# Second layer in Strassen form for all groups, banks seeded by copies, and a searched order of instructions, in an attention and gated two-layer kernel

## The chip, the cores and the metric

One core of a Trainium2 chip runs the whole program. The metric is the device time of one execution in microseconds (us), lower is better. TensorE does the matmuls, VectorE and ScalarE the element-wise work, GpSimd some conversions and the issue of stores, SyncE the issue of most loads. In profile lines they are PE (and PEld for its weight loads), DVE, ACT, POOL and SP; a q behind a name (SPq) is that engine's sequencer, which issues transfers. Most executions of a kernel agree within some tenths of a per cent; single ones are slower, and a run over 1.5% above the fastest of its kernel counts as slow.

## The reference

```python
# q, k, v: (8 batches, 8 heads, 576 positions, 64), float32
def phi(x, c, s):                        # c, s: cosine and sine of the position
    r = np.maximum(x, 0.0)
    return np.concatenate([r * c, r * s], axis=-1)
kv  = einsum('bhsf,bhsd->bhfd', k_p, v)           # k_p = phi(k), q_p = phi(q)
z   = sum(k_p, axis=2)
num = einsum('bhsf,bhfd->bhsd', q_p, kv)
den = einsum('bhsf,bhf->bhs', q_p, z) + 1e-6
x   = (num / den), heads merged                   # (4608, 512)
h   = x @ w_in                                    # 512 -> 2048
out = (h * cos(h)) @ w_out                        # 2048 -> 512
```

The 4608 rows are taken in nine groups of 512: the first 512 positions of each of the eight batches, and one group "r" gathered from what is left over of all batches. Attention of a batch makes the x of its group. Layer 1 is x @ w_in with the gate, layer 2 is the product with w_out.

## The kernel before

Every piece of work is an operation with the engines that may do it, an estimated time for each, a priority, dependences, and slots of buffer rings that it takes or gives back. A list scheduler, run while the program is built, picks the next operation and fixes both its engine and its place. On the chip each engine then does its own line strictly in that order.

```python
t0, e0 = min((c[0], c[1]) for c in cand)           # earliest start over all candidates
t, _, us, o, _ = min((c for c in cand if c[1] == e0 and c[0] <= t0 + self.EPS),
    key=lambda c: (c[4] if e0 == "DMA" else 0.0, c[3].prio, c[0]))
```

A batch begins with its features, phi of k and q. They read buffers of which there is one per tensor (k, q, v), so the next batch's loads start when the last feature has read its buffer. For the first batches VectorE or ScalarE does a k feature:

```python
kf[(t, g)] = op({"A": 0.68, "V": 0.46} if cut or not g else {"A": 0.68},   # cut: batches 0, 1
    (2, b, 1), lambda e, t=t, g=g: feat(e, b, "k", t, g),
    deps=[ka, land[(b, "k", 0)]], rel=[sl["raw_k"]])
```

Layer 2 of group 0 is plain, 64 matmuls of 512 columns:

```python
def layer2_plain(base):
    for t in T:                                     # four tiles of 128 rows
        h1 = op({"PE": 1.73}, base(t, 0), lambda t=t: plain2(t, range(NJT // 2)),
                deps=d + w_land[NG:NG + NG // 2], acq=[s], rel=[g_slot[0]])
        h2 = op({"PE": 1.73}, base(t, 1), ..., deps=[h1] + w_land, rel=[g_slot[0]])
        c = op({"A": 0.6, "V": 0.69}, ..., ev, deps=[h2] + ...)     # copy to the output tile
```

The other eight groups use a Strassen form (Winograd's): seven products of half size in place of eight, in three PSUM banks X, Y and Z, with sums of gates (s) and of weights (WT) made by VectorE. The first product (X) is needed in three results, so it is saved, and added to the others from there:

```python
p1 = product(0, [], gates, [sX])
e1 = op({"A": 0.6}, EV, lambda e: cp(e, part(g, "s1"), ps[(g, "X")]), deps=[p1], acq=[s1])
p6 = product(1, wsum, S_(1), [sY])
e6 = op({"V": 0.69}, EV, lambda e: add(part(g, "u2"), g, "Y", "s1"), deps=[p6, e1], ...)
# ... p2, p7, p5, p4, p3, with three more additions of this kind on VectorE
```

Of the kernel before, what the change touches and what calls it, by code (L numbers as in the profile page):

```python
# [14 lines left out]

class Slot:


    def __init__(self, ring, n=1):
        self.ring, self.left, self.end = ring, n, 0.0  # L20


def flat(x):
    return tuple(z for y in x for z in flat(y)) if isinstance(x, tuple) else (x,)


class Op:
    def __init__(self, alts, prio, fn, deps, lat, acq, rel, at):
        self.alts, self.prio, self.fn, self.deps, self.lat = alts, flat(prio), fn, deps, lat
        self.acq, self.rel, self.at, self.end = acq, rel, at, None  # L30


class Plan:


    SEM, EPS = 0.08, 0.1

    def __init__(self, rings):
        self.ops, self.free = [], {r: [0.0] * n for r, n in rings.items()}
# [6 lines left out]
    def run(self, cold=0.0):  # L46
        users, wait = {}, {}
        for o in self.ops:
            wait[o] = len(o.deps)
            for d in o.deps:  # L50
                users.setdefault(d, []).append(o)
        ready = [o for o in self.ops if not wait[o]]
        clock, order = {}, []
        while ready:
            cand = []
            for o in ready:
                t = max([o.at] + [d.end + d.lat for d in o.deps])
                if any(not self.free[s.ring] for s in o.acq):
                    continue
                for s in o.acq:  # L60
                    t = max(t, min(self.free[s.ring]))
                for e, us in o.alts.items():
                    cand.append((max(t, clock.get(e, 0.0)), e, us, o, t))
            if not cand:
                left = [(o.prio, o.alts, [s.ring for s in o.acq if not self.free[s.ring]],
                         [(d.prio, d.alts) for d in o.deps if d.end is None][:3])
                        for o in self.ops if o.end is None]
                raise RuntimeError("no operation can start: " + repr(left[:12]))
            t0, e0 = min((c[0], c[1]) for c in cand)
            t, _, us, o, _ = min(  # L70
                (c for c in cand if c[1] == e0 and c[0] <= t0 + self.EPS),
                key=lambda c: (c[4] if e0 == "DMA" else 0.0, c[3].prio, c[0]))
            if e0 == "PE" and t < cold:
                us *= 1.7
            for s in o.acq:
                self.free[s.ring].remove(min(self.free[s.ring]))
            o.end = t + us + (self.SEM if us else 0.0)
            clock[e0] = t + us
            for s in o.rel:
                s.left, s.end = s.left - 1, max(s.end, o.end)  # L80
                if not s.left:
                    self.free[s.ring].append(s.end)
            order.append((t, len(order), o, e0))
            ready.remove(o)
            for u in users.get(o, ()):
                wait[u] -= 1
                if not wait[u]:
                    ready.append(u)
        assert len(order) == len(self.ops)
        order.sort(key=lambda x: x[:2])  # L90
        return [(o, e) for _, _, o, e in order]
# [3 lines left out]
def kernel(  # L95
# [50 lines left out]
    WT = cpool.tile([P, 4, HJ, HM], F16, name="WT")  # L146
# [4 lines left out]
    kvzs, kps, qps, qTs, qTr, x16s, xts, gts, sms, osts, ps = ({} for _ in range(11))  # L151
    T, T1 = range(NT), range(NT + 1)
    HS = [slice(0, HB), slice(HB, H)]
    RING = {"m1": 4, "l2": 2, "at": 1}
# [20 lines left out]
    def feat(eng, b, name, t, g, hs=ALLH):  # L175
        dst = (kps if name == "k" else qps)[b][:, t, hs, g, :]
        src, sc = raw[name][:, hs, t, :], CS[:, b % 2, g, t:t + 1]
        if eng == "A":
            nc.scalar.activation(out=dst, in_=src, func=AF.Relu, scale=sc)  # L179
        else:  # L180
            (nc.vector if eng == "V" else nc.gpsimd).tensor_scalar(  # L181
                out=dst, in0=src, scalar1=0.0, scalar2=sc, op0=ALU.max, op1=ALU.mult)
# [10 lines left out]
    def q_tiles(b):  # L193
        qps[b] = apool.tile([P, NT + 1, H, 2, D], F16, name=f"qp{b}", tag="qp", bufs=1)

    def qT_tiles(b):
        qTs[b] = apool.tile([P, NT, H, P], F16, name=f"qT{b}", tag="qT", bufs=1)

    def qR_tiles(b):
        qTr[b] = apool.tile([P, H, P], F16, name=f"qR{b}", tag="qR", bufs=2)  # L200

    def qT(b, t):
        return qTs[b][:, t] if t < NT else qTr[b]
# [27 lines left out]

    def ratio(b, t, tile_, hbs):
        nb, h0 = len(hbs), hbs[0] * HB
        den = apool.tile([P, nb, HB], F32, name=f"den{b}_{t}", tag="den")
        nc.vector.tensor_scalar_add(out=den, in0=tile_[:, :, :, D], scalar1=1e-6)
        rec = apool.tile([P, nb, HB], F32, name=f"rec{b}_{t}", tag="rec")
        nc.vector.reciprocal(out=rec, in_=den)  # L237
        if hbs[0] == 0:
            x16s[(b, t)] = apool.tile([P, H, D], F16, name=f"x16{b}_{t}", tag="x16", bufs=4)
# [19 lines left out]

    def transposes(key, tag, srcs_, **kw):  # L260
# [4 lines left out]
    def q_src(b, t, h):  # L265
        return qps[b][:, t, h].rearrange("p g d -> p (g d)")

    def q_trans_dma(b, t):
        nc.sync.dma_start_transpose(  # L269
            out=qT(b, t), in_=qps[b][:, t].rearrange("p h g d -> p (h g d)"))  # L270
# [12 lines left out]

    def sin(key):
        ps[("ch", key)] = apool.tile([P, SM], F32, name="ch", tag="ch", bufs=4)
# [4 lines left out]
    def gate(key, dst):  # L290
        m = ps[key]
        nc.vector.tensor_tensor(  # L292
            out=dst, in0=m, in1=ps[("ch", key)].rearrange("p (j s) -> p j s", s=m.shape[2]),
            op=ALU.mult)
# [4 lines left out]
    def s_tiles(g):  # L299
        sms[g] = gpool.tile([P, 2, HJ, HT], F16, name=f"s{g}", tag="s")  # L300

    def sums(g, c, n):
# [3 lines left out]
        a12, s1, s2 = gv[:, 1, js, 0:HT], sms[g][:, 0, js], sms[g][:, 1, js]  # L306
        out, in0, in1, op = ((s1, a21, a22, ALU.add), (s2, s1, a11, ALU.subtract),
                             (a21, a11, a21, ALU.subtract), (a12, a12, s2, ALU.subtract))[n]
        nc.vector.tensor_tensor(out=out, in0=in0, in1=in1, op=op)  # L309

    def weight_sum(n):
        wv = w_out_sb.rearrange("p (j e) m -> p e j m", e=2)
        b11, b12 = wv[:, 0, :, 0:HM], wv[:, 0, :, HM:Dm]
        b21, b22 = wv[:, 1, :, 0:HM], wv[:, 1, :, HM:Dm]
        x, y = ((b12, b11), (b22, WT[:, 0]), (b22, b12), (b21, WT[:, 1]))[n]
        nc.vector.tensor_tensor(out=WT[:, n], in0=x, in1=y, op=ALU.subtract)

    def prod(g, n, c):
        gv = gts[g].rearrange("p (j e) s -> p e j s", e=2)
        sv, wv = sms[g], w_out_sb.rearrange("p (j e) m -> p e j m", e=2)  # L320
        lo, hi, ml, mh = slice(0, HT), slice(HT, SM), slice(0, HM), slice(HM, Dm)
        bank, first, lhs, rhs = (
            ("X", True, gv[:, 0, :, lo], wv[:, 0, :, ml]),
            ("Y", True, sv[:, 1], WT[:, 1]),
            ("X", False, gv[:, 1, :, lo], wv[:, 1, :, ml]),
            ("Y", False, gv[:, 0, :, hi], WT[:, 2]),
            ("Z", True, sv[:, 0], WT[:, 0]),
# [469 lines left out]
```

## Time and profile before

| | before |
|---|---|
| the 3 runs | 301.12, 303.61 and 308.33 us (the last counts as slow) |
| span of the profiled run | 298.7 us |
| TensorE busy | 280.1 us, 94% |
| VectorE, ScalarE, GpSimd busy | 233.7, 175.6, 102.0 us |

This is the chain of waits of the kernel before from 27 to 54 us (start, length, what):

```profile
27.75 9.18 PE M L279 x84
36.93 6.91 PE M L376 x32
...
47.45 3.45 PE M L376 x16
50.90 1.21 PE KV L219 x40
52.11 0.41 PE N L228 x12
52.52 1.74 PE M L376 x8
```

Only TensorE stands in it: layer 1 of group 0 (L279), its plain layer 2 (L376), and in the middle of that, at 50.90, the kv matmuls of batch 1. The rows of batch 1's k features (name, count, shortest, median and longest ns, first and last start) show who prepared them:

```profile
L181 DVE TENSOR_SCALAR kp<-km,CS x6: 470/482/617, 45.5 to 48.3; 128x512 f16<-128x512 f32 x6
L179 ACT ACTIVATE kp<-km,CS x4: 706/706/722, 45.5 to 47.7; 128x512 f16<-128x512 f32 x4
```

Six on VectorE and four on ScalarE begin when k has landed (45.4), are done at 48.7, and TensorE never waits for them.

### The profile page before, as it was taken

The page shows a single profiled execution, that of the slowest core. Times are in us where ns is not written, and L with a number is a line of the kernel's source. Part 1 is how long each engine was busy: PE and PEld are TensorE (multiplying, and loading weights), DVE is VectorE, ACT ScalarE, POOL GpSimd, SP SyncE. Part 2 cuts the span into 40 slices and gives each one's busy share as a digit, 9 for nine tenths or more (in the row PEclk, how much of TensorE's full clock was granted, in tenths as well). Part 3 has the DMA queues.
Part 4 walks back from the last instruction along what each step waited for, and adds up shares of the span by engine and source line. Part 5 has one row for each costly group of instructions (what it writes and reads, how often), then busy time and mean ns, then how long its engine had stood idle before and what let it go on. Part 6 is the DMA issues. An engine that isn't in the chain of part 4 may idle for free.

```text
span 298.7 us, 6583 instructions
## 1 busy us (share of the span) xinstructions
PE 280.1 (94%) x2565; PEld 201.3 (67%) x2565; DVE 233.7 (78%) x450; ACT 175.6 (59%) x303; POOL 102.0 (34%) x107
## 2 busy tenths in 40 slices
PE   8879999899969987999979999999999999999993
PEld 8768856688855555566646666776666666566782
DVE  1878888899995798887869798987786786768661
ACT  2846748599379797679489497634433443443210
POOL 1370004396191686287077194011002001100500
PEclk9979999999999999999999999999999999999998
DMA  7799995897899999999999999715202100200213
GB/s 218 264 163 203 204 362 183 279 308 120 273 274 235 356 232 169 283 278 203 322 256 202 238 369 195 141 47 151 35 0 94 48 1 32 111 2 0 91 52 140
DMA packets 77086, 53.29 MB, mean 178 GB/s; under 512 B 46080, under 2 KB 74752, under 8 KB 77056
## 3 DMA queue, kind: packets, MB, share of 16 engines
q1 hardware_dynamic: 69760, 39.73, 55.2%
q0 software_dynamic: 6848, 12.59, 16.6%
q10 hardware_dynamic: 448, 0.57, 0.5%
q8 instruction: 20, 0.33, 0.5%
q14 instruction: 10, 0.08, 0.1%
HBM read 36.74 MB, written 9.44 MB: 155 GB/s over the span
## 4 chain that ended last, share of the span: by engine, by line
PE 55%; DMA 16%; DVE 10%; POOL 5%; SPq 5%; ACT 4%; issue 3%; ACTq 0%; DVEq 0%
PE M L279 26%; DMA vm<-in_v_dram 13%; PE PY L337 8%; PE PZ L337 6%; PE PX L337 5%; PE M L376 5%; POOL qp L181 4%; DMA qm<-in_q_dram 3%; PE KV L219 2%; DVE g L292 2%; SPq L171 2%; DVE x L241 2%; PE TP L263 2%; DVE s L309 2%; SPq L269 1%
## 5 line engine op out<-in xcount | busy, mean ns | idle before, releaser
L279 PE MATMUL M<-xT,w_in_sb 128*128 128x512 f16 (+1 forms) x640 | 120.2, 336 | 2.9 <-ACT xT L159 2.6
L286 ACT ACTIVATE ch<-M 128x512 f32<-128x512 f32 x144 | 84.9, 595 | 60.8 <-PE M L279 58.7
L292 DVE TENSOR_TENSOR g<-M,ch 128x512 f16<-128x512 f32 x128 | 85.8, 687 | 27.0 <-ACT ch L286 26.1
L279 PEld LDWEIGHTS <-w_in_sb 128*128 128x128 f16 x704 | 67.3, 98 | 46.6 <-issue 3.1
L181 POOL TENSOR_SCALAR qp<-qm,CS 128x512 f16<-128x512 f32 x29 | 60.0, 2074 | 31.0 <-DMA qm<-in_q_dram 27.0
L337 PEld LDWEIGHTS <-g 128*128 128x128 f16 x560 | 54.1, 98 | 11.5
L369 POOL DMA_DIRECT2D out_dram<-ost x14 | 7.8, 558 | 98.6 <-DVE ost L351 42.5
L179 ACT ACTIVATE kp<-km,CS 128x512 f16<-128x512 f32 x52 | 35.1, 715 | 0.2
L179 ACT ACTIVATE qp<-qm,CS 128x512 f16<-128x512 f32 x40 | 26.9, 713 | 11.9 <-DMA qm<-in_q_dram 11.9
L337 PE MATMUL PX<-w_out_sb,g 128*128 128x256 f16 x224 | 27.6, 273 | 0.0
L241 DVE TENSOR_TENSOR x<-N,rec 128x512 f16<-128x512 f32 (+1 forms) x44 | 26.1, 594 | 1.7 <-DVE rec L237 0.2
L337 PE MATMUL PY<-WT,g 128*128 128x256 f16 x224 | 27.2, 273 | 0.0
L337 PEld LDWEIGHTS <-s 128*128 128x128 f16 x224 | 21.4, 98 | 7.1 <-DVE s L309 2.8
L161 POOL CAST V<-vm 128x512 f16<-128x512 f32 (+1 forms) x22 | 13.9, 664 | 15.9 <-DMA vm<-in_v_dram 15.9
L228 PE MATMUL N<-kvz,qT 128*128 128x65 f16 x256 | 14.7, 196 | 2.3 <-DVE x L241 2.1
L228 PEld LDWEIGHTS <-qT 128*128 128x128 f16 x256 | 12.6, 100 | 6.1 <-issue 3.5
L337 PE MATMUL PY<-WT,s 128*128 128x256 f16 x112 | 14.1, 273 | 2.2 <-DVE s L309 2.2
L181 DVE TENSOR_SCALAR kp<-km,CS 128x512 f16<-128x512 f32 x28 | 15.5, 590 | 0.3 <-DMA km<-in_k_dram 0.2
L292 DVE TENSOR_TENSOR gr<-M,ch 128x512 f16<-128x512 f32 x16 | 10.9, 689 | 5.7 <-ACT ch L286 5.5
L219 PE MATMUL KV<-V,kp 128*128 128x65 f16 x320 | 12.9, 196 | 2.5 <-DVE kp L181 0.7
L279 PE MATMUL M<-xR,w_in_sb 128*128 128x512 f16 x64 | 15.1, 379 | 0.0
L219 PEld LDWEIGHTS <-kp 128*128 128x128 f16 x320 | 11.7, 99 | 4.7 <-issue 2.4
(70 smaller groups left out, 287.7 us busy)
## 6 DMA issues: line engine op xcount, KB each, us to landing
out_dram<-ost POOLq DMA_DIRECT2D x28, 256.0 KB, 4.1
qm<-in_q_dram SPq DMA_DIRECT2D x8, 640.0 KB, 5.3
km<-in_k_dram SPq DMA_DIRECT2D x8, 640.0 KB, 7.0
qm<-in_q_dram SPq DMA_DIRECT2D x8, 512.0 KB, 5.8
km<-in_k_dram SPq DMA_DIRECT2D x8, 512.0 KB, 8.8
vm<-in_v_dram SPq DMA_DIRECT2D x6, 640.0 KB, 8.1
vm<-in_v_dram SPq DMA_DIRECT2D x6, 512.0 KB, 8.9
w_in_sb<-in_moe_w_in_dram POOLq DMA_DIRECT2D x4, 512.0 KB, 9.0
```

The costliest lines, as they stand in the source:

```text
L161: (nc.vector if eng == "V" else nc.gpsimd).tensor_copy(out=out, in_=in_)
L179: nc.scalar.activation(out=dst, in_=src, func=AF.Relu, scale=sc)
L181: (nc.vector if eng == "V" else nc.gpsimd).tensor_scalar(out=dst, in0=src, scalar1=0.0, scalar2=sc, op0=ALU.max, op1=ALU.mult)
L219: nc.tensor.matmul(tile_[:, n, hh, :], lhsT=kps[b][:, t, h].rearrange("p g d -> p (g d)"), rhs=V1[:, t, h, :], start=(t == 0), stop=(t == NT))
L228: nc.tensor.matmul(tile_[:, n, hh, :], lhsT=qT(p, t)[:, h, :], rhs=kvzs[p][:, h, :], start=(i == 0), stop=(i == len(parts) - 1))
L241: nc.vector.tensor_tensor(out=dst, in0=tile_[:, :, :, 0:D], in1=rec.unsqueeze(3).broadcast_to((P, nb, HB, D)), op=ALU.mult)
L279: nc.tensor.matmul(ps[key][:, n, :], lhsT=w_in_sb[:, c, j * P:(j + 1) * P], rhs=x[:, c, s0:s1], start=(c == 0 and n == 0), stop=(c == NCT ...
L286: nc.scalar.activation(out=ps[("ch", key)], in_=ps[key].rearrange("p j s -> p (j s)"), func=AF.Sin, bias=math.pi / 2.0, scale=1.0)
L292: nc.vector.tensor_tensor(out=dst, in0=m, in1=ps[("ch", key)].rearrange("p (j s) -> p j s", s=m.shape[2]), op=ALU.mult)
L337: nc.tensor.matmul(ps[(g, bank)][:, i, :], lhsT=lhs[:, j, i * P:(i + 1) * P], rhs=rhs[:, j], start=(first and i == 0 and j == 0), stop=(j ...
L369: e0.dma_start(out=five[:, t0:t0 + 2, :], in_=blocks(ost, n))
L376: nc.tensor.matmul(ps[("M2", t)], lhsT=gts[0][:, j, t * P:(t + 1) * P], rhs=w_out_sb[:, j, :], start=(j == 0), stop=(j == NJT - 1))
```

## The change

The intent: fewer matmuls (group 0 in Strassen form too), less VectorE work for the evacuation of the products (a copy of X into the bank Y, onto which the next products are added), finer buffer rings for q, and an order of all operations found offline by annealing in place of the scheduler. The description of the change also says that GpSimd runs no two-input operation; that was true of the kernel before as well. Layer 1 stays plain; code for a Strassen form of it is there, unused, but three of its sums over w_in are still computed.

```diff
-    def run(self, cold=0.0):
-        ... (the list scheduler)
+    def run(self):
+        return [(self.ops[int(x.rstrip("VAG"))], x.lstrip("0123456789"))
+                for x in ORDER.split()]
+ORDER = """
+115 22 25 230 180 184 883 818 24 229 342 21 40A 41V 42A 60 43V 44A 61V 62 45A 63V 64 38A 32V 36V
+ ... (1351 tokens: operation number and engine)
 # rings
-    "qp": 1, "qT": 1, "x16": 4, "ch": 4, "s": 2
+    "qp": 4, "qT": 4, "x16": 3, "ch": 3, "s": 3          # q by single blocks, x16 one fewer
 # evacuation of X into Y
-        p1 = product(0, [], gates, [sX])
-        e1 = op({"A": 0.6}, EV, lambda e: cp(e, part(g, "s1"), ps[(g, "X")]), ...)
+        def y_seed(e):
+            if g == 0:
+                cp(e, part(g, "p1"), ps[(g, "X")])
+            else:
+                ps[(g, "Y")] = ppool.tile([P, 2, HM], F32, name="SD", tag="l2", bufs=2)
+                cp(e, ps[(g, "Y")], ps[(g, "X")])
+        y1 = op(CP, EV, y_seed, deps=[p1], acq=[sY] if g else [q1])
 # group 0
-    layer2_plain(lambda t, n: (1, 1, t, n))
+    wsum1 = []
+    for n in range(3):                                   # read by nobody: layer 1 is plain
+        wsum1.append(op(WSUM, (1.6, n), lambda e, n=n: w_in_sum(e, n), ...))
+    layer2(0, lambda i: (1, 1, i))
```

Besides, the last product of the last group is split into two halves, each with its own copy and stores, and some denominators and value conversions go to other engines.

## The prediction

> **What bounds the kernel now.** I read the busy table and the 40 slices first, then the window table, then the chain of waits, then the wait lists, then the groups by shape. The busy table:
>
> ```profile
> PE 280.1 (94%) x2565; PEld 201.3 (67%) x2565; DVE 233.7 (78%) x450; ACT 175.6 (59%) x303; POOL 102.0 (34%) x107
> ```
>
> TensorE (PE) is far ahead, but its ends are modelled, so I priced it by start-to-start times. The chain of waits of the last third gives them, since PE follows itself there without a hole:
>
> ```profile
> 46.56 0.89 PE TP L263 x16
> ...
> 117.90 1.21 PE KV L219 x40
> ...
> 209.59 1.75 PE PY L337 x16
> 211.34 1.73 PE M L279 x8
> ```
>
> So a 512-column matmul costs 1.73/8 = 0.216 us, a 256-column one 1.75/16 = 0.109, a 65-column attention matmul 1.21/40 = 0.030, a transpose 0.89/16 = 0.056. From the first KV matmul at 13.13 us (timeline) the counts are 512 of the first kind, 1152 of the second, 640 of the third and 100 of the fourth: 110.7 + 125.6 + 19.2 + 5.6 = 261.1 us of work. PE's last matmul ends at about 293.95, so 280.8 us pass: PE has 19.7 us of holes. The same subtraction by stretch puts 6.1 of them at 13 to 30, 2.4 at 50 to 60, 6.5 at 80 to 120, 2.7 at 140 to 160, 1 at 160 to 200 and none after 200. The window table shows the same places (columns: width, then busy of PE, PEld, DVE, ACT, POOL):
>
> ```profile
> 13.00:30.00 17.00, 13.92 (x163) 11.84 (x162) 13.86 (x42) 9.89 (x19) 7.28 (x12) 0.90 1.01 163
> 30.00:50.00 20.00, 20.00 (x149) 13.04 (x147) 17.81 (x30) 13.68 (x23) 3.89 (x10) 1.00 1.05 279
> 50.00:60.00 10.00, 8.68 (x136) 6.69 (x134) 7.61 (x31) 6.07 (x13) 2.79 (x3) 1.00 0.69 217
> 60.00:80.00 20.00, 20.00 (x229) 17.85 (x227) 19.30 (x36) 15.50 (x28) 12.18 (x9) 1.00 0.90 219
> 80.00:120.00 40.00, 34.39 (x348) 23.04 (x346) 33.12 (x63) 32.32 (x56) 25.92 (x17) 1.00 1.12 256
> ...
> 200.00:280.00 80.00, 80.00 (x558) 53.24 (x556) 58.91 (x93) 33.04 (x56) 7.71 (x16) 1.00 0.16 50
> ```
>
> From 200 on PE is saturated: only fewer matmuls help there. Before 200 it waits now and then for attention, and PE's wait list names single waits, not a steady one:
>
> ```profile
> PE N L228 <- DVE x L241: 2.8, 2, 2.1
> PE M L279 <- ACT xT L159: 2.6, 1, 2.6
> PE PY L337 <- DVE s L309: 2.2, 2, 1.6
> PE TP L263 <- ACT xT L159: 1.5, 4, 0.5
> ```
>
> (Total us, times, longest.) Each is a place where an engine's order was unlucky. After the last matmul come one VectorE (DVE) addition, 293.98 to 294.67, and the last stores, to 298.73.
>
> **What the Trainium skill says.** "TensorE: Matmul & The Clock Gate", section "Wait — 56ns, not 53.3ns?", gives N / 2.4 GHz + about 2.5 ns warm, which is 215.8 and 109.2 ns: the trace agrees (216 and 109). "VectorE: DVE Perf Modes", section "The perf-mode tier table", holds any tensor_tensor with a PSUM operand at one element a cycle: the additions on PSUM take 687 ns for 512 elements, and a PSUM copy 678, so turning an addition into a copy on DVE saves nothing; only moving it to ScalarE (ACT) does (595 ns). "PSUM — Partial Sum Buffer", section "The four PSUM rules", says that ACT and DVE writes do not set the has_written bits, so a seeded bank is added to only where an earlier matmul left them set. The trace before has no seeding. The change fits the rule: group 0 alone starts its Y bank with a matmul and adds the first product by an instruction, and its products leave both banks of that ring fully written. "GPSIMD Engine Reference", section "Engine selection", makes two-input work on GpSimd (POOL) about twice as slow; the trace has none there, before or after, so that phrase of the change removes nothing.
>
> **The change part by part** (counts from the built order of both kernels, durations from the rows of before).
>
> *Group 0's second layer becomes Strassen.* 64 matmuls of 512 columns (13.8 us) give way to 112 of 256 (12.2): PE 261.1 -> 259.5 us, -1.6. It brings 8 sums to DVE (about 0.70 us each, 5.6).
>
> *Evacuation by seeding.* 40 additions on PSUM (27.5 us of DVE) become 19 (13.1), and 10 copies on ACT with 2 on DVE plus 8 saved first products become 5 + 17 + 2 half + 8 on ACT and 14 on DVE (9.5 us). ACT +12 copies and two half ones, 8 us; DVE -14.4 + 9.5 - 1.4 = -6.3.
>
> *Rest of DVE.* Three sums over w_in of 128x2048 are still built, though the plain first layer never reads them: +3.7 us of dead work at 1.22 each. The weight sums are cut in halves, about +0.5. Seventeen denominators go to ACT, -2.7; six value casts leave, -2.6; five q and one k feature come, +3.1. Sum over all parts: 5.6 - 6.3 + 3.7 + 0.5 - 2.7 - 2.6 + 3.1 = +1.3, so DVE stays near 235.
>
> *ACT and POOL.* ACT: 15 k features leave (-10.7), 4 q features (+2.9), copies +8, seventeen denominators (estimate 0.2 each, +3.5), four value casts (+2): near 181. POOL: 29 features become 34 at 2.07 us, near 112. None becomes the bound by sum.
>
> *Finer rings.* The feature tile of q was one buffer of five blocks, so the next batch's features waited for all five transposes; it becomes four single-block buffers, likewise the transposed tile. The row of POOL features had 27.0 us idle behind q loads, so this slackens the loop of features, transposes and loads. Worth nothing by itself; it lets the order be better.
>
> *Searched order.* This is the main term, since it goes at the 19.7 us. Nothing in the profile gives its size; I take it by stretch. 13 to 30: 6.1 -> 5, because the first loads end this wait. 50 to 60: 2.4 -> 3.5, worse: up to the end of batch 1's ratios DVE must now do about 4 us more (group 0's sums and the dead w_in sums come before), and it had 17.81 of 20 busy at 30 to 50. 60 to 120: 6.7 -> 2.5, single waits that an order can move. 140 to 200: 3.7 -> 1. After 200: 0 -> 0.6, because the last group's seed copy and two additions sit in line between its products (0.69 each, with about one 0.87 us product to cover each). Sum 19.7 (with 0.8 of scatter) -> 12.6 to 13.4: -6.7.
>
> *The tail.* The last evacuation becomes a half copy (estimate 0.4 us, from the 387 ns of the 128x260 ACT copies) in place of 0.69, and the last store is 128 KB, whose median landing is 2.0 us against 2.4 and 3.0 for 256 KB: -1.0. Two filler matmuls at PE's end (0.43) lie beside the store.
>
> Sum: -1.6 - 6.7 - 1.0 = -9.3 us of the 298.7 us span, 289.4, a ratio of 0.969. On the median of 303.61 that is 294; the median holds one slow draw (308.33), and on the mean of the other two, 302.4, it is 293. The search could do better than my cautious split, so I say 292.
>
> **The rivals.** *The order removes nearly all holes.* For it: holes are few and single, ACT and POOL have room, and DVE's average after 200 is 59 of 80. Holes of 4 us would give 261 - 1.6 + 13.1 + 4 + 3.1, about 280 us of span, 285 measured. Against: an order searched offline rests on fixed durations, and DMA landings vary (v loads took 7 to 12 us in the chain).
>
> *DVE becomes the bound before 120.* It has 19.30 of 20 busy at 60 to 80, more work is put just before, and a fixed order makes every engine wait for a late one. The gain of the order would go into PE waits on group 0's sums and batch 1's ratios: holes stay near 19, the rest gives -2.6, some 301 measured: same.
>
> *DMA sets attention's pace.* The mean share of the queues is 1.1 of capacity at 80 to 160 and a v load of 10.5 us is in the chain. The bytes do not change, so waits on loads would stay. Against: the transfers end at about 190 while PE works on to 294, so they are ahead on average. This too would keep about 6 us of holes, some 298 measured.
>
> *A longer dependency through the seed.* The copy must end before the next product of X and before the first of Y. With first-layer matmuls between, it is hidden; if the order packed it too tightly, 9 groups of 0.5 us would add 4.5.
>
> **Range and chances.** 292, with 286 to 299 for 8 in 10: the lower end has holes of some 7 us, the upper nearly all of them kept. Faster by over 2% means under 297.5: holes must fall by about 4 us or more together with the two sure terms. I give that 0.77, within 2% 0.20, slower 0.03, the last only if the fixed order falls out of step.
>
> **What would show it.** Right: 1264 matmuls of 256 columns and 448 of 512; PE's idle time between 60 and 200 at half or less; DVE near 235, ACT near 181; the end of PE to the end of the span about 1 us shorter. Wrong: PE waiting on sums or ratios of DVE between 40 and 70 for more than 4 us; waits of PE on seeded banks in every group; waits on loads that are as long as before. If the holes stay and the time falls, or they go and it does not, my account of the bound is wrong.

## The result, and the profile after

The changed kernel took 313.53 us (median of 4, 312.30 to 313.61) against 302.4 for the kernel before (mean of its two fast runs, 301.12 and 303.61; 305.67 and 308.33 count as slow): ratio 1.036, 95% interval 1.0275 to 1.0444. It is slower. (A ratio is the mean time of one kernel's fast runs over that of the other's fast runs in the same rounds, so it is not quite the quotient of the medians.) The profiled execution: span 310.2 us, 11.5 more than before.

The busy table after:

```profile
PE 281.8 (91%) x2615; PEld 205.1 (66%) x2615; DVE 233.6 (75%) x440; ACT 180.3 (58%) x326; POOL 111.7 (36%) x114
```

The sums are those foreseen: VectorE 233.6 (235 predicted), ScalarE 180.3 (181), GpSimd 111.7 (112). The work did not grow, so the time is in holes of TensorE. I took them as in the prediction: the time between the starts of two matmuls, less the price of the first by its width; a hole is counted in the stretch in which that first matmul begins. The whole program, from its first matmul, is then 270.4 us of work and 22.4 of holes before, 269.2 and 35.6 after:

| stretch, us | holes before | predicted after | measured after |
|---|---|---|---|
| 0 to 13 | 3.1 | not given | 4.6 |
| 13 to 30 | 6.1 | 5 | 6.3 |
| 30 to 50 | 0.1 | no change | 5.4 |
| 50 to 60 | 2.4 | 3.5 | 2.8 |
| 60 to 120 | 6.7 | 2.5 | 4.5 (3.3 to 80, 1.2 after) |
| 120 to 140 | 0.0 | no change | 1.5 |
| 140 to 200 | 3.7 | 1 | 8.4 (6.2 of it after 160) |
| 200 to the end | 0.2 | 0.6 | 2.1 |

The window table of the changed kernel for the stretches that answer to those shown of before:

```profile
30.00:50.00 20.00, 16.32 (x139) 13.73 (x138) 14.79 (x25) 9.16 (x17) 1.42 (x6) 0.91 1.07 265
50.00:60.00 10.00, 8.09 (x111) 6.79 (x109) 8.83 (x17) 9.74 (x18) 2.21 (x7) 1.00 0.01 2
...
80.00:120.00 40.00, 39.43 (x417) 29.08 (x416) 35.70 (x66) 26.43 (x52) 18.71 (x16) 1.00 1.02 235
```

From 80 to 120 PE is busy 39.43 of 40 where it had 34.39: the search did fill the holes that it was made for. From 30 to 50 PE fell from 20.00 to 16.32, and so did VectorE (17.81 to 14.79) and ScalarE (13.68 to 9.16). No engine is the bound there; they wait for each other. From 50 to 60 ScalarE has 9.74 of 10, and the transfers move 2 GB/s where they moved 217: no load of batch 2 is under way. PE's list of waits names the largest:

```profile
PE N L256 <- DVE x L276: 5.7, 3, 4.7
PE PX L430 <- DMA w_out_sb<-in_moe_w_out_dram: 3.0, 1, 3.0
PE TP L303 <- ACT qp L209: 2.1, 3, 1.2
PE KV L247 <- ACT kp L209: 1.9, 4, 1.0
```

The chain of waits says how these hang together. It is the answer to the six lines of before, from 20 to 68 us:

```profile
20.63 22.09 DMA w_out_sb<-in_moe_w_out_dram
...
42.77 1.34 PE PX L430 x6
...
44.13 0.61 ACT p L189
...
50.98 1.22 ACT kp L209 x2
...
53.42 3.68 ACT kp L209 x6
...
57.15 0.66 PE KV L247 x16
...
59.96 1.23 ACT qp L209 x2
...
61.21 0.60 SPq L201
...
61.85 5.71 DMA qm<-in_q_dram
```

Where only PE stood before, there is now the last quarter of w_out, a copy of X by ScalarE, eight k features of batch 1 on ScalarE, batch 1's kv matmuls, its last q features, the issue of batch 2's q load at 61.2 (51.4 before), and that load. The rows of the features:

```profile
L209 ACT ACTIVATE kp<-km,CS x8: 711/712/714, 50.9 to 56.4; 128x512 f16<-128x512 f32 x8
L211 DVE TENSOR_SCALAR kp<-km,CS x2: 481/482/482, 54.2 to 54.6; 128x512 f16<-128x512 f32 x2
```

Two on VectorE, eight on ScalarE, the last done at 57.1 in place of 48.7. Layer 1 of group 1 began at 66.4 us, not 58.3. Most of these 8.1 us stay: layer 1 of group 2 began at 97.6 against 89.9, 7.7 later.

The 5.4 us of holes at 30 to 50 come before all this. From start to start, 3.2 of them are the wait for the last quarter of w_out, which the first product of group 0 reads, 1.0 is a wait for the copy of X, and the remaining 1.2 are matmuls that the trace shows at half the clock (0.5 from 42.9 to 46.3 us), right after the long wait.

### The profile page after: what moved, and what is told of

Its sections match the earlier page's. It is cut to its first block, busy times and chain, and to the rows that moved or that the text cites. A ratio compares the mean times of both kernels' runs of the same rounds, so it can differ in the third digit from the quotient of the medians.

```text
span 310.2 us, 6724 instructions
## 1 busy us (share of the span) xinstructions
PE 281.8 (91%) x2615; PEld 205.1 (66%) x2615; DVE 233.6 (75%) x440; ACT 180.3 (58%) x326; POOL 111.7 (36%) x114
## 4 chain that ended last, share of the span: by engine, by line
PE 60%; DMA 20%; ACT 6%; DVE 3%; issue 1%; SPq 1%; POOL 0%; ACTq 0%; DVEq 0%
PE M L319 29%; PE SD L430 11%; PE PX L430 9%; DMA xT<-x 9%; DMA w_out_sb<-in_moe_w_out_dram 7%; PE PZ L430 7%; PE KV L247 3%; ACT kp L209 3%; DMA km<-in_k_dram 2%; DMA qm<-in_q_dram 2%; PE N L256 1%; ACT qp L209 1%; DVE g L332 1%; DVE x L276 1%; ACT ch L381 1%
## 5 line engine op out<-in xcount | busy, mean ns | idle before, releaser
L430 PEld LDWEIGHTS <-g 128*128 128x128 f16 x640 | 61.9, 99 | 20.4 <-issue 7.3
L211 POOL TENSOR_SCALAR qp<-qm,CS 128x512 f16<-128x512 f32 x20 | 42.0, 2106 | 40.7 <-DMA qm<-in_q_dram 22.8
L430 PE MATMUL PX<-w_out_sb,g 128*128 128x256 f16 x256 | 34.4, 280 | 4.1 <-DMA w_out_sb<-in_moe_w_out_dram 3.0
L465 POOL DMA_DIRECT2D out_dram<-ost x14 | 7.8, 560 | 76.2 <-ACT ost L189 55.2
L209 ACT ACTIVATE qp<-qm,CS 128x512 f16<-128x512 f32 x44 | 29.9, 713 | 6.9 <-DMA qm<-in_q_dram 6.9
L211 POOL TENSOR_SCALAR kp<-km,CS 128x512 f16<-128x512 f32 x14 | 29.3, 2105 | 3.1 <-DMA km<-in_k_dram 2.7
L430 PEld LDWEIGHTS <-s 128*128 128x128 f16 x256 | 24.5, 98 | 4.7 <-issue 0.2
L209 ACT ACTIVATE kp<-km,CS 128x512 f16<-128x512 f32 x37 | 24.5, 711 | 2.5 <-DMA km<-in_k_dram 2.5
L430 PE MATMUL PZ<-w_out_sb,g 128*128 128x256 f16 x128 | 16.6, 273 | 0.0
L430 PE MATMUL PZ<-WT,s 128*128 128x256 f16 x128 | 16.3, 273 | 0.0
L430 PE MATMUL SD<-WT,g 128*128 128x256 f16 x112 | 14.5, 273 | 0.7 <-ACT ost L189 0.7
```

Of the source, the lines that this page charges most:

```text
L209: nc.scalar.activation(out=dst, in_=src, func=AF.Relu, scale=sc)
L211: (nc.vector if eng == "V" else nc.gpsimd).tensor_scalar(out=dst, in0=src, scalar1=0.0, scalar2=sc, op0=ALU.max, op1=ALU.mult)
L430: nc.tensor.matmul(ps[(g, bank)][:, i, :], lhsT=lhs[:, j, i * P:(i + 1) * P], rhs=rhs[:, c * HJ // 2 + j], start=(first and i == 0 and j = ...
L465: e0.dma_start(out=five[:, t0:t0 + 2, :], in_=blocks(ost, n))
```

## The experiments

Eighteen kernels ran. All outputs are right. I name them by their labels and give the median and the ratio to the kernel before. The runs came in several calls, in which the fast runs of the kernel before had medians of 301.8 to 304.7 us, so where two kernels of different calls are compared, the difference of the ratios (1% is 3.0 us) is the fairer one; I give it beside the medians. An interval that reaches below 1.02 leaves open whether a kernel is slower by 2%; one that stays above 1 says that it is slower. In the diffs, letters behind an operation number are engines (A ScalarE, V VectorE).

### First round: which part costs

**greedy**: the changed kernel's operations, ordered by the scheduler of before.

```diff
-class Plan: ... return tokens of ORDER
+class Plan: ... the list scheduler of the kernel before
```

> The changed kernel's operations, tiles and rings, but the order made by the scheduler of the kernel before instead of the searched list. Theory A (the searched order does not fit the chip): 293 to 302 us, PE holes after 13 us at 20 or less. Theory B (the parts themselves, Strassen in group 0, seeding, dead sums, overload DVE early): 308 or more. Theory C (the x16 ring cut from four to three buffers stalls DVE on transposes): 305 to 310, with DVE waiting on transposes for several us again.

326.5 us (three fast runs), ratio 1.083 [1.0742, 1.0923]. The profiled execution itself: 1642 us, so its trace is not used. The searched order is worth some 13 us to these operations (326.5 to 313.5; 14 by the ratios); the operations themselves are what the old scheduler cannot place.

**x16_4**: one more buffer for the normalised x, in the searched order.

```diff
-"x16": 3,
+"x16": 4,
```

> The changed kernel with the x16 ring at four buffers again, the same searched order. Theory C: the 4.7 us PE wait on a ratio at about 172 us and the 5.4 us DVE wait on a transpose go, 305 to 308 us. Theory A in its general form (any slip makes a hole somewhere): part of it comes back elsewhere, 309 to 312. Theory B: 312 to 314.

309.96 us, 1.029 [1.0212, 1.0368]: 3.6 us less by the medians, 2 by the ratios. In the changed kernel the largest single wait lies at 160 to 180 us. PE's and VectorE's lists of waits for that window:

```profile
PE N L256 <- DVE x L276: 4.7, 1, 4.7
```

```profile
DVE x L276 <- DMA xT<-x: 5.4, 1, 5.4
```

VectorE could not write x because all three buffers were held by transposing transfers, and PE waited behind it. With four buffers that wait is nearly gone, but the holes of the stretch only fell from 6.2 to about 5.2 (and those from 180 to 200 rose by 1.2), because in ScalarE's line a k feature now waits for its load with cosines behind it (lists of ScalarE and PE, same window):

```profile
ACT kp L209 <- DMA km<-in_k_dram: 4.2, 1, 4.2
```

```profile
PE M L319 <- DVE g L332: 3.0, 2, 2.4
```

So its gain need not be from this stretch at all: layer 1 of group 1 began 1.8 us earlier (64.6) in this run. The interval overlaps that of the changed kernel.

**no_dead**: the three unread sums over w_in left out.

```diff
-lambda e, n=n: w_in_sum(e, n)
+lambda e: None
```

> The changed kernel without the three sums over w_in that nobody reads, the same searched order. Theory B: 309 to 311, since DVE gets 3.7 us back where batch 1 needs it. Theories A and C: 312 to 314.

309.53 us, 1.0278 [1.0193, 1.0363]: 4.0 us less by the medians, 2.5 by the ratios. The three sums of 1.22 us stand in VectorE's line from 55 us on, between a transposed copy, sums and ratios that others wait for, so they are not beside other work. The intervals of the two kernels overlap here too. Layer 1 of group 1 begins at 63.6, 2.8 earlier, but some of that is luck: the last quarter of w_out landed at 41.1 in this run, at 42.7 in that of the changed kernel, and batch 1's features, which stand ahead of the dead sums, ended at 54.2 instead of 57.1.

**strassen0**: the kernel before, with Strassen form in group 0. The weight sums that it needs got an earlier priority (0.9 for 1.5), and the scheduler ran anew.

```diff
-    layer2_plain(lambda t, n: (1, 1, t, n))
+    layer2(0, lambda i: (1, 1, i))
```

> The kernel before with one part of the change alone: group 0's second layer as Strassen with the old additions, order by the old scheduler. Theory B: 307 us or more. Theories A and C: 300 to 305, near the kernel before; PE work falls by 1.6 us and some of it comes back as waits on DVE's sums between 40 and 60 us.

309.4 us, 1.0252 [1.016, 1.0344]. The part that was to remove 1.6 us of matmuls costs 7.6 us with the order that the scheduler made for it. Seven features go to ScalarE, the last ends at 53.8, layer 1 of group 1 begins at 65.6. TensorE's two waits from 30 to 60 us lie before that: 3.6 us for a q feature of batch 1, whose transposes stand in its line amid group 0's products, and 1.4 for w_out.

### Second round: do the parts add, and are the seeds innocent

**plain0**: no dead sums, and group 0 plain, its pieces set into the slots that the searched order has for the seven products.

```diff
-lambda c=c: prod(g, n, c)
+lambda c=c: prod(g, n, c) if g else plain0(n, c)     # sums and additions of group 0: nothing
```

> The changed kernel with group 0's second layer plain again in the same places of the searched order, and without the dead sums (w_out's four sums get a place of their own). Theory D (Strassen in group 0 needs all of w_out and its sums early, in a stretch in which TensorE waits for loads anyway, so it saves nothing and adds waits): 302 to 306, against 309.5 without the dead sums alone. If the loss is in the rest of the order instead: 309 to 311.

314.03 us, 1.032 [1.0264, 1.0376]. By this alone Strassen in group 0 would be cleared. But the trace shows that the order holds the old assignment fast. VectorE's timeline (start, length, what, and in brackets the idle time before it and its cause):

```profile
44.09 0.48 DVE L211 TENSOR_SCALAR qp<-qm,CS 128x512 f16<-128x512 f32 x1
53.05 0.69 DVE L191 COPY ost<-M 128x512 f32<-128x512 f32 x1 [8.49 <-PE M L475]
```

VectorE stands idle for 8.49 us behind one copy that must wait for a matmul, while eight k features lie in ScalarE's line and end at 58.6. The sums are gone and nothing took their place.

**both**: no_dead and x16_4 together.

```diff
-lambda e, n=n: w_in_sum(e, n)
+lambda e: None
-"x16": 3,
+"x16": 4,
```

> The changed kernel without the dead sums and with four x16 buffers. If the two losses add: 305 to 307. If the wait on transposes only moves to the next one in line: 308.5 to 310, as without the dead sums alone.

311.05 us, 1.0246 [1.0191, 1.0302]: 0.3% and 0.4% below the ratios of the two, inside the intervals. That the gains add is not shown.

**seed**: the kernel before with banks seeded by copies in groups 1 to 8, group 0 plain, order by the scheduler.

```diff
-            ("Y", True, sv[:, 1], WT[:, 1]),
+            ("Y", False, sv[:, 1], WT[:, 1]),       # onto the copied X
```

> The kernel before with seeded banks and copies for groups 1 to 8 alone (group 0 plain, old scheduler). Theory E (the seed chain X to copy to Y puts waits of PE into each group): 308 or more, PE waits named SD or PX after copies. Theory D: within 1% of before, 300 to 306, since first-layer matmuls lie between.

305.12 us, 1.001 [0.9962, 1.0059]. Seeding, with the order that the scheduler makes for it, neither costs nor gains; layer 1 of group 1 begins at 58.3 as before.

**greedy_nows**: greedy without the dead sums.

```diff
-        wsum1.append(op(WSUM, (1.6, n), lambda e, n=n: w_in_sum(e, n), ...))
```

> The changed kernel's operations without the dead sums, order by the old scheduler, for a trace that isn't in the slow state. 319 to 324 if the dead sums cost 3 to 5 us there too; its holes after 200 us and on seeded banks show whether the loss of 326 is of the old scheduler's order of the new products (PE waits on SD and PZ in every group) or early.

316.71 us (2 runs), 1.0406 [1.0349, 1.0462]: 9.7 us less than greedy by the medians, 12.9 by the ratios, far over the 3.7 us of the dead sums. The scheduler ran anew, so the rest of the order differs too.

### Third round: is it batch 1's features

**dve_load**: the kernel before plus eight sums over group 0's gates, 5.5 us of VectorE, into a buffer nobody reads.

```diff
+                for n in range(4):
+                    op({"V": 0.69}, (1, 0, c, n), lambda e, c=c, n=n: dead(c, n), deps=d)
```

> The kernel before plus eight sums of 128x1024 over group 0's gates on VectorE, written to a scratch buffer that nobody reads, 5.5 us of VectorE between 36 and 48 us and nothing for TensorE to wait for; group 0 stays plain. If VectorE's load ahead of batch 1's features is the cause: more k features of batch 1 go to ScalarE, they end near 52 to 54, the first layer of group 1 starts at 62 to 66 instead of 58, ratio 1.010 to 1.025. If the cause is TensorE's own waits on sums and weights in group 0: first layer of group 1 at 58 to 60, ratio 0.995 to 1.008.

307.08 us, 1.014 [1.0052, 1.0227]. TensorE has nothing to wait for in these sums, and its list shows no such wait. Still seven features went to ScalarE, the last ended at 51.3, and layer 1 of group 1 began at 61.3, 3 us late. Load on VectorE ahead of batch 1's features costs time without any sum that TensorE waits for, 4.2 us by the ratio, less than strassen0's 7.6. (Here too the scheduler ran anew.)

**kfeat**: plain0 with six k features of batch 1 on VectorE, ahead of the copy that waits.

```diff
-... 264V 265A ...
+... 264V 251V 252V 253V 255V 256V 260V 265A ...
```

> The plain0 kernel (searched order, group 0's second layer plain in the same slots, no dead sums) with one move: the six k features of batch 1 that stand late in line (four of them on ScalarE) go to VectorE, ahead of the output copy for which VectorE waited 8.49 us. Theory A (the shift of 8 us arises because batch 1's k features end at 57 to 58 us instead of 49): features now end near 50, the loads of batch 2 go out near 54 instead of 64, the first layer of group 1 starts near 61 instead of 69, and the time falls from 314.0 to 306 to 309. Rival B (the shift is TensorE's wait on the weights of w_out and the place of the products in the searched line): the first layer of group 1 still starts at 67 or later and the time stays within 312 to 316.

311.06 us, 1.0264 [1.0194, 1.0334]: 3.0 us less than plain0 by the medians, 1.7 by the ratios, where I expected 5 to 8. The four features left on ScalarE stood behind a copy that waited and ended at 57.2.

**hyb_plain** and **hyb_str**: everything up to the first product of group 1 ordered by the scheduler, the rest in the searched order; group 0 plain in one and in Strassen form in the other.

```diff
-        return [tokens of ORDER]
+        return [scheduled prefix] + [tokens of ORDER from the first product of group 1]
```

> The changed kernel's operations without dead sums, group 0 plain, four buffers for x16; everything up to the first product of group 1 is ordered by the scheduler of before, everything after it keeps the searched order. Theory A (the start costs the time, the searched order helps from 80 us on): the first layer of group 1 starts at 58 to 61, the holes at 80 to 120 us stay near 1 to 3, and the time is 298 to 304. Rival (the searched order fits only its own start): new waits of TensorE right after the seam and at 80 to 160, time 308 to 315.

> The same as hyb_plain but with Strassen in group 0: this pair differs in group 0's second layer alone, with the same rest of the order. If Strassen in group 0 is what costs (its sums on VectorE push batch 1's features to ScalarE, its first product needs the second half of w_out early), this is 4 to 8 us slower than hyb_plain, and the first layer of group 1 starts 4 to 7 us later. If the searched order of the start was what cost, the pair is equal within 2 us.

312.18 us, 1.0312 [1.0227, 1.0397], and 312.29 us, 1.0287 [1.0215, 1.0358]. Both missed. I had left the durations of the Strassen sums in the scheduler's model of hyb_plain, so in both it believed VectorE full and put all ten k features on ScalarE (done at 57.6 and 54.7). The pair doesn't compare what it was made to compare.

### Fourth round: the same, properly controlled

**kfeat2**: plain0 with all ten k features on VectorE.

```diff
+... 264V 251V 252V 253V 254V 255V 256V 257V 258V 259V 260V ...
```

> The plain0 kernel with all ten k features of batch 1 on VectorE, ahead of the copy that it waits for (kfeat left four on ScalarE, where they ended at 57 us behind a copy that waited). Theory A (late features shift everything): features end near 52, the KV matmuls of batch 1 are over by 56, loads of batch 2 go out near 57, the first layer of group 1 starts near 62, time 305 to 309. Rival (the shift comes from the rest of ScalarE's line, q features and transposed copies): first layer of group 1 still at 65 to 67, time 310 to 312 as in kfeat.

307.65 us, 1.0185 [1.0135, 1.0234]: faster than plain0 by 6.4 us of medians, 4.1 by the ratios, for a move of ten instructions to 45 us. VectorE's timeline, to be held against plain0's:

```profile
45.84 4.75 DVE L211 TENSOR_SCALAR kp<-km,CS 128x512 f16<-128x512 f32 x10 [1.90 <-DMA km<-in_k_dram]
52.42 0.69 DVE L191 COPY ost<-M 128x512 f32<-128x512 f32 x1 [1.83 <-PE M L475]
```

The features fill the hole, the copy comes no later than it did (52.42 against 53.05), and layer 1 of group 1 begins at 62.9 instead of 68.7.

**hyb2**: no dead sums, four buffers for x16, group 0 plain with true durations; the scheduler's order up to the first matmul of group 1, the searched order from there on.

```diff
+        layer2_plain(lambda t, n: (1, 1, t, n))
+        return [scheduled prefix] + [tokens of ORDER from the first matmul of group 1]
```

> The changed kernel's operations without dead sums, group 0 as in the kernel before, four buffers for x16; everything up to the first matmul of group 1 ordered by the scheduler of before with the true durations of a plain group 0 (it splits batch 1's k features 6 and 4), everything after it in the searched order. Theory A: first layer of group 1 at 58 to 60, holes at 80 to 120 us stay at 1 to 3, time 299 to 305, which would be level with the kernel before or better. Rival (the searched order loses wherever the real durations differ from its own, not just at the start): the start is good but new waits after 120 us bring it to 307 or more.

302.3 us, 0.9993 [0.9947, 1.004]: level with the kernel before, and 11 us faster than the changed kernel. Features 6 and 4 again, layer 1 of group 1 at 61.2. What the search gains at 80 to 160 us (4.6 us of holes, 9.3 before) goes into a few us in other places, among them 2.4 at 160 to 180 and 1.5 after 200.

**str0_k**: strassen0 with batch 1's k features on VectorE alone and ahead of the sums in priority.

```diff
-{"A": 0.68, "V": 0.46} ..., (2, b, 1)
+{"V": 0.46} if b == 1 else ..., (0.3, b, 1) if b == 1 else (2, b, 1)
```

> The kernel before plus Strassen in group 0 (as strassen0, 309.4), with batch 1's k features on VectorE alone and ahead of group 0's sums in priority. Theory A: the features end near 51 instead of 54, the first layer of group 1 starts near 62 instead of 66, time 305 to 308. Rival (TensorE's waits on the delayed sums and on w_out in group 0 are what cost): the sums come 3 to 4 us later, group 0's products end later, the first layer of group 1 starts at 65 to 68 and the time is 308 to 312.

313.45 us, 1.0364 [1.0305, 1.0423], a miss both ways. The start came as theory A had it (features done at 52.6, layer 1 of group 1 at 61.9), yet the time rose. The scheduler reordered everything after, and 17 us of holes stand between 120 and 200 us, two of them waits for x of 8.6 us together. An experiment that lets a list scheduler run anew changes more than its edit.

### Last round: Strassen in group 0 with the rest held fixed

**hyb2_str**: as hyb2, but group 0 in Strassen form, batch 1's k features ahead of its sums.

```diff
-    layer2_plain(...)
+    layer2(0, lambda i: (1, 1, i))
-                    (2, b, 1), lambda e, t=t, g=g: feat(e, b, "k", t, g),
+                    (0.3 if b == 1 else 2, b, 1), lambda e, t=t, g=g: feat(e, b, "k", t, g),
-            wsum[(n, c)] = op({"Vp": 0.7}, (1.5, c, n), ...)
+            wsum[(n, c)] = op({"Vp": 0.7}, (0.9, c, n), ...)
```

> The same as hyb2 (302.3) but with Strassen in group 0; batch 1's k features stand ahead of group 0's sums, split between VectorE and ScalarE, and all from the first matmul of group 1 on is the same searched order. If only late features cost: features end near 50, the first layer of group 1 starts at 60 to 62, time 300 to 304, within 1% of hyb2. If the start cannot hold Strassen's 8 sums, its weight sums and the early second half of w_out at all: the first layer of group 1 starts at 64 or later and the time is 305 to 310. I lean to the second, since the copies, sums and features of both must share 20 us of VectorE and ScalarE.

311.47 us (median of 4 fast runs of 6; 315.03 and 316.30 count as slow), 1.0281 [1.0217, 1.0346]. Against hyb2 this is 9.2 us by the medians, 8.7 by the ratios and 9.8 by the spans (310.5 and 300.7), for the start alone, since all from group 1's first matmul on has one order in both: the traces show the same line on every engine. TensorE's holes from 30 to 80 us are 6.2 in hyb2 and 14.9 here, those from 140 to 200 4.3 and 7.2: part of the loss of the start shows only later. The windows of hyb2, then of hyb2_str:

```profile
30.00:50.00 20.00, 18.71 (x138) 12.15 (x137) 16.62 (x32) 12.83 (x23) 2.84 (x8) 1.00 1.04 271
50.00:66.00 16.00, 14.28 (x170) 10.45 (x168) 11.41 (x41) 7.81 (x15) 7.86 (x6) 0.89 0.66 207
66.00:80.00 14.00, 13.96 (x157) 12.54 (x156) 13.41 (x25) 12.32 (x23) 7.21 (x6) 1.00 0.61 144
```

```profile
30.00:50.00 20.00, 14.16 (x125) 11.51 (x123) 16.63 (x29) 13.18 (x23) 3.17 (x8) 0.99 0.99 253
50.00:66.00 16.00, 15.10 (x188) 13.39 (x188) 10.30 (x32) 10.50 (x17) 2.08 (x6) 0.80 0.10 25
66.00:80.00 14.00, 11.46 (x107) 9.92 (x106) 10.04 (x23) 9.39 (x18) 11.54 (x8) 1.00 1.06 335
```

In the second window PE is busy for 14.28 and 15.10 us, but hyb2 moves 207 GB/s there and hyb2_str 25: batch 2's loads go out at 52.9 and at 62.8. VectorE is busy 16.62 and 16.63 in the first. Here the k features were early (done at 48.3) and there was no wait on w_out. So neither of these two is the whole cause. Now batch 1's q features were late (the last at 62.8): they stood in ScalarE's line behind copies that waited for TensorE, whose transposes stood behind products of group 0. The batch was late with them. And more than half of the loss had come before 50 us (holes of 7.3 in the first window, 1.7 in hyb2). The largest entry of TensorE's list of waits from 30 to 70 us is none of the Strassen form as such:

```profile
PE KV L306 <- POOL V L250: 2.8, 4, 1.2
```

The scheduler had put batch 1's kv matmuls ahead of more than half of group 0's products in TensorE's line, where they waited for values that GpSimd converted late; then the trace shows half clock from 49.5 to 56.3 us. How a Strassen start without this wait would do is not tested.

**hyb2_tail**: hyb2 with the two halves of the last product issued together, ahead of both copies.

```diff
-1506 1503A 1507 1504 817 1508A 1505 1509 1510
+1506 1507 1503A 1508V 1504 1505 817 1509 1510
```

> hyb2 with the four half matmul runs of the last product issued together, ahead of the two half copies, of which the second goes to VectorE. If TensorE's 0.8 us between the halves is on the path to the end: span 0.5 to 0.9 us shorter than hyb2, ratio to before 0.995 to 0.998. If the copy and the store hide it: no change, ratio 0.998 to 1.002. It would be level with or slightly better than before, not over 1% better.

303.05 us (6 runs), 0.9997 [0.9953, 1.0041]. TensorE's wait of 0.64 us between the halves is gone in the trace; the time is the same within the interval. No version that ran beats the kernel before.

**after_k**: the changed kernel itself, ten k features of batch 1 on VectorE, ahead of group 0's remaining sums and additions.

```diff
+... 264V 251V 252V 253V 254V 255V 256V 257V 258V 259V 260V ...
```

> The changed kernel with one edit: batch 1's ten k features all on VectorE, right behind the q feature that it does at 47.8 us, ahead of group 0's remaining sums and additions (in kfeat2 the same move, with group 0 plain, was worth 6.4 us). If VectorE had room, as with group 0 plain: features end near 53, first layer of group 1 at 61 to 63, time 306 to 309. If Strassen's sums and additions, which now come 4 us later, are as much on the path as the features: first layer of group 1 at 65 to 67, time 311 to 315. I lean to the second.

314.49 us (5 runs), 1.0388 [1.0334, 1.0441]: nothing gained. VectorE's timeline and PE's list of waits for 44 to 62 us:

```profile
46.91 5.02 DVE L211 TENSOR_SCALAR kp<-km,CS 128x512 f16<-128x512 f32 x10
...
52.65 0.69 DVE L332 TENSOR_TENSOR PY<-PY,p 128x512 f32<-128x512 f32 x1
...
53.44 0.70 DVE L332 TENSOR_TENSOR PZ<-PY,p 128x512 f32<-128x512 f32 x1
```

```profile
PE PY L430 <- DVE PZ L332: 3.6, 1, 3.6
```

The same ten instructions whose move was worth 4 to 6 us with group 0 plain now push the additions of group 0 back, and TensorE waits 3.6 us for one of them (0.8 in the changed kernel), with batch 1's kv matmuls behind it in its line. In this order VectorE has no place for both; that no order has one is not shown.

The starts side by side, for all kernels that share the searched order from group 1 on (hyb_plain and hyb_str from its first product on; hyb2_tail starts as hyb2). The four hybrids, x16_4 and both have a fourth buffer for x16; after, after_k and x16_4 still have the dead sums:

| kernel | group 0 | k features done | batch 2's q load issued | layer 1 of group 1 begins | ratio to before |
|---|---|---|---|---|---|
| hyb2 | plain | 50.4 | 52.9 | 61.2 | 0.999 |
| kfeat2 | plain | 50.6 | 58.0 | 62.9 | 1.019 |
| no_dead | Strassen | 54.2 | 58.3 | 63.6 | 1.028 |
| x16_4 | Strassen | 55.2 | 59.3 | 64.6 | 1.029 |
| both | Strassen | 56.8 | 60.9 | 66.2 | 1.025 |
| kfeat | plain | 57.2 | 61.1 | 66.3 | 1.026 |
| after | Strassen | 57.1 | 61.2 | 66.4 | 1.036 |
| hyb2_str | Strassen | 48.3 | 62.8 | 66.6 | 1.028 |
| hyb_str | Strassen | 54.7 | 62.9 | 63.7 | 1.029 |
| after_k | Strassen | 51.9 | 63.0 | 68.2 | 1.039 |
| plain0 | plain | 58.6 | 63.6 | 68.7 | 1.032 |
| hyb_plain | plain | 57.6 | 66.5 | 67.8 | 1.031 |

The end of the k features does not fix the time (hyb2_str). The q load waits for the last q feature, and the q features stand in line with the k features, the copies and the sums. The two best kernels are early in both other columns, but beyond them no column sets the ratio: kfeat2 and no_dead issue that load within 0.3 us of each other and differ by 0.9%, and hyb_plain issues it 5.3 us after the changed kernel at a ratio that is no worse.

## Why the prediction was wrong, point by point

**What bounds the kernel.** Right after 200 us and right that holes are the thing to count. Wrong in taking all of them for single unlucky waits before looking at what stands beside TensorE when it has none. At 30 to 50 us there was no hole to gain, but much to lose: the plain layer 2 of group 0 was the cover under which VectorE and ScalarE prepared batch 1. (The matmul prices hold, though two of the four lines that they are taken from, at 46.56 and 117.90, are not of the last third of the chain.)

**Group 0's layer 2, -1.6.** The matmul counts are as said; the work fell by 1.2 us, since the two filler matmuls at the end add 0.4. This term failed, not in its size but in standing alone. The saved matmuls lie in the stretch 30 to 58 us, and the Strassen form there replaces a run of matmuls that needs nobody by products that wait for w_out, copies and sums. strassen0 shows +2.5% for this part with an order of its own, the pair hyb2 and hyb2_str 9 to 10 us for the start in which it stands.

**The step that failed: the start, "50 to 60: 2.4 -> 3.5", and 30 to 50 taken for unchanged.** The term named a right reason, VectorE having some 4 us more to do before batch 1's ratios, and sized it at 1.1 us within ten microseconds. Between 50 and 60 the holes came to 2.8, less than said; but over 30 to 80 us they went from 2.7 to 11.5 us (0.1, 2.4 and 0.2 against 5.4, 2.8 and 3.3), +8.8. About half of that is a wait that the prediction did not have: 3.2 us for the last quarter of w_out, with 1.2 of matmuls at half clock behind it. For the rest, the prediction priced the extra work as length; its cost was in whom it displaces. The k features went to ScalarE, where one takes 0.71 us instead of 0.48 and stands behind waiting copies. They ended 8.4 us late, the q features stood behind them, and the loads of batch 2 hung on those. dve_load and kfeat2 show that late features cost time; after_k shows that with Strassen form in group 0 moving them alone does not mend it. The sign that the prediction set for this failure, over 4 us of TensorE waiting for VectorE between 40 and 70 us, did not come: those waits add to 1.5 us (0.8, 0.5, 0.2). The waits were for ScalarE and for w_out, since the work had moved there.

**The searched order, -6.7 in all.** Right at 80 to 120 (6.5 to 1.2), which is the gain that it was credited with. The rest did not come. 140 to 200 was to fall from 3.7 to 1 and rose to 8.4. The largest wait there comes with a term that the prediction didn't have, the ring of x16 being one buffer shorter (5.4 us on VectorE). But that the ring is the cause is not shown: with the fourth buffer that wait goes and the holes from 140 to 200 are 8.9 us (x16_4). With the ring and the order of this stretch the same, a plain start has 4.3 and a Strassen start 7.2 (hyb2, hyb2_str), so a part follows from the start. Net, holes grew by 13.2 us (22.4 to 35.6) where they were to fall by 6.7.

**The rest of VectorE, +1.3.** The sums are right to 1.4 us. The dead w_in sums, booked as load without effect, cost 2.5 to 4 us by no_dead, though not clear of noise; they stand in the same critical stretch.

**Evacuation by seeding.** Right that the seeds don't cost: seed is at 1.001, and TensorE waits only 0.4 us for a seeding copy in the whole changed kernel.

**The tail, -1.0.** From the end of the last product to the end of the span it was 4.8 us before and is 4.7 after. The half copy is short, but the second half of the product waits 0.7 us for the first's copy, and hyb2_tail shows that taking this away doesn't move the time either.

**The rivals.** "VectorE becomes the bound" came nearest: it saw that group 0's sums and batch 1 compete. It expected holes as before and the gain eaten, not a loss, and by its own sign, VectorE full, it is wrong: at 30 to 50 us VectorE was less busy than before. None of my rivals was a late batch. "DMA sets the pace" had the right place in one respect, that a load of batch 2 is in the chain; but it is late because it is issued late.

Sum: work -1.2 and holes +13.2 to the end of TensorE's last matmul, which is a filler now, and from there to the end of the span 4.3 us for 4.8, -0.5: +11.5 us, as measured in the span.

What stays open: how the 9 to 10 us of hyb2_str divide between sums, copies, half clock and the place of the kv matmuls in TensorE's line; whether another order of a Strassen start would lose less; and why the scheduler's own later orders differ by several us (str0_k, greedy).

## What to carry to other kernels

Before moving work into a stretch where the main engine has no holes, list what the other engines do under that cover and what is issued when they finish; a batch that starts late stays late if the rest is saturated. With engines that work in order, price an added instruction by what stands behind it in its line. To compare two starts, hold the order of everything after them fixed: a scheduler that is run again changes more than the edit.

## What the Trainium skill lacked or had wrong

- "Perfetto Trace Analysis", section "Identifying the Most-Contended Engine", goes by occupancy for VectorE, ScalarE and GpSimd, and for TensorE by its rate and the busy time of weight loads. Here VectorE 233.7 and 233.6 us, ScalarE 175.6 and 180.3, weight loads 201.3 and 205.1 say nothing of an 11.5 us longer span. The next section, "Optimization Strategy", to look at gaps in the stretch concerned and at what blocks them, led to the answer. Neither speaks of an engine that is idle because one waiting copy stands first in its line (8.49 us in plain0), nor of what saturated stretches hide.
- "TensorE: Matmul & The Clock Gate", section "What's actually happening", has the clock halved after about 3.4 us of idle time. Here half pace followed a wait of 3.0 us: the next six 256-column matmuls took 1.34 us, the later ones 0.213 each from start to start against 0.109, and the window 30 to 50 has a granted clock of 0.91. In x16_4, at 173.7 us, a wait of 2.4 us was followed by 512-column matmuls of 0.427 us against 0.216.
- "PSUM — Partial Sum Buffer", section "The four PSUM rules", calls 0 the only seed that is safe either way. That is right but no ban: eight groups were seeded with a product in each execution of the changed kernel and of seed, and the results were correct in all runs; by what the same section explains, the bits were left set by earlier matmuls.
- "DMA: Bandwidth & Descriptors", section "Anatomy of one DMA — SWDGE (gpsimd) path", gives about 2.0 us of fixed cost and the bytes over 436 GB/s, for 512 KB an estimate of 3.2 us. The last quarter of w_out took 22.09 us from issue to landing, beside other loads. No page says how to estimate that.
- No page gives the time of a 128x512 float32 copy from one PSUM bank to another. It was 582 ns on ScalarE and 700 on VectorE, near that of a copy out of PSUM (598 and 683).
